# A token mixer in two groups of token tiles, with its sums added to u^T once a group

## The chip, the cores and the metric

The kernel runs on one core of a Trainium2 chip. The metric is device time in microseconds (us) of one execution, lower is better. Five engines work side by side, each through its own instructions in order: PE (TensorE, matrix products), DVE (VectorE), ACT (ScalarE), POOL (GpSimd) and SP (SyncE, which issues the transfers). They wait for each other on semaphores.

## The reference

Three stages follow each other. The first is a delta-rule attention over 768 tokens, 8 heads of width 48 and 4 batches; the other two work on its output `x` of shape (4, 768, 384):

```python
theta = x @ w_theta
zr, zi = x * np.cos(theta), x * np.sin(theta)
y = np.einsum('ts,bsd->btd', w_tok_r, zr) + np.einsum('ts,bsd->btd', w_tok_i, zi)
u = x + y
x = u + np.maximum(u @ w_ch, 0.0)
mu = np.mean(x, axis=-1, keepdims=True)
var = np.mean((x - mu) ** 2, axis=-1, keepdims=True)
xn = (x - mu) / np.sqrt(var + 1e-06) * g_ln
out = x + np.maximum(xn @ w_ch1, 0.0) @ w_ch2
```

The weights of the last two stages arrive in 64-bit floating point. Products are made in a 32-bit form that keeps fewer bits, so each operand is split into a high part and the rest (hi and lo), and three products (hi·hi, hi·lo, lo·hi) stand for one.

## The kernel before, in words

The attention takes the first 226 us. Then comes the mixing, 24 steps long. A step is one pair (batch b, token tile s) of the list `MIX`; a token tile is 128 tokens. The list goes through all six tiles of batch 0, then of batches 1, 2 and 3, the last one in the order 5, 4, 3, 2, 0, 1.

For a step, PE multiplies the tile's zr and zi (hi and lo) with the tile's token weights `w` and adds to six sums `y` in PSUM, three in each half of the step (L902 `mix`). A sum has 128 channels by 384 tokens; the six hold u^T of one batch. The sums of one batch run over its six steps. After the last of them DVE adds each to `uT` (L921), in which ACT has put x^T before (L849), and the next batch starts in the same three plus three PSUM buffers.

The preparation of later tiles runs ahead inside the step, between its halves: `theta(i+2)` on PE, `transpose(i+3)` on PE, `angles(i+2)` on DVE (`kk`, `nf`), `copies(i+3)` (`xh` on ACT, `xl` on DVE, x^T to `uT` on ACT), `sines` and `cosines` on ACT. At the start of step i, `turn(i+1)` makes the products with x (`zf`, one on POOL, one on DVE), the high parts `zh` (ACT) and the rest `zl` (POOL).

The same engines convert the 64-bit weights, half a token tile (a unit of 128 x 768) at a time, in the class `Weights`. A unit passes: transfer to `raw`, absolute value on ACT (L759), two instructions on DVE called the clamp here (L765, L766), two called the low pair (L775, L776), the cast of the high part on ACT (L789), and the subtraction for the low part (L794), which `add(..., split=)` gives to POOL or to DVE. `pump()` moves the units one stage on; the lists `PA` and `PB` say how many pumps a step makes, before its first and before its second half. In the first steps there are two a step, later one. Tiles 0 and 1 are loaded from late in the attention on, tiles 2 to 5 in steps 0 to 5, just ahead of their use. After them come twelve `stash` units (FFN weights, scaled by g on POOL and stored to DRAM), and `w_ch`.

The FFN stage takes eight halves j of a batch (384 tokens). Before half j can start, `pre(j)` runs eight pieces: `parts` (split of u), three `ch` (the w_ch product), `total`, `centre`, `square` with a second total, and `rstd`. For j = 0 they are placed in the mixing's last steps and the FFN's first ones, by the small dictionaries in the loop of `build`; the psum of a first product `ph` comes from the same buffers as the sums `y` of a step's first half.

Of the kernel before, what the change touches and what calls it, by code (L numbers as in the profile page):

```python
# [6 lines left out]
F32 = mybir.dt.float32  # L7
F32R = mybir.dt.float32r
# [3 lines left out]
ALU = mybir.AluOpType  # L12
# [650 lines left out]
C = 384  # L663
KB = 3
# [135 lines left out]
class Mixer:  # L800
# [19 lines left out]
    def load_w(self, s, wtok, pool, wts, w=None):  # L820
        w = self.W[s] = w or [pool.tile([128, 4, C], F32R, name=f"w{s}_{i}") for i in range(2)]
        for q in range(2):
            wts.add(("w", s, q), wtok[s, q], w[0][:, 2 * q:2 * q + 2], w[1][:, 2 * q:2 * q + 2])

    def trans(self, i):

# [11 lines left out]
    def copies(self, i, soon=1):  # L838
        nc = self.nc
        b, s = MIX[i]  # L840
        ps = self.XT
        xh = self.tp.tile([128, KB, 128], F32R, name="xh")
        xl = self.tp.tile([128, KB, 128], F32R, name="xl")
        nc.scalar.copy(out=xh, in_=ps)
        for k in range(2):
            if k == soon:
                nc.vector.tensor_tensor(out=xl, in0=ps, in1=xh.bitcast(F32), op=ALU.subtract)
            else:
                nc.scalar.copy(out=self.uT[b][:, :, 128 * s:128 * s + 128], in_=ps)  # L849
# [49 lines left out]

    def mix(self, i, half, yp):  # L900

        nc = self.nc  # L902
        b, s = MIX[i]
        zh, zl = self.Z[i]
        first, last = i % 6 == 0, i % 6 == 5
        qs = range(3 * half, 3 * half + 3)
        if first:
            for q in qs:
                self.Y[q] = yp.tile([128, C], F32, name="y", tag="h" if q < 3 else "acc")
        for ps in (((zh, 0), (zl, 0)), ((zh, 1),)):  # L910
            for q in qs:
                k, h = q // 2, q % 2
                for ri in range(2):
                    for l, w in ps:
                        nc.tensor.matmul(self.Y[q], l[:, ri, 128 * k:128 * k + 128], self.W[s][w][:, 2 * ri + h],  # L915
                                         start=(first and w == ri == 0 and l is zh), stop=(last and w == ri == 1))
        if last:
            for q in qs:
                k, h = q // 2, q % 2
                o = self.uT[b][:, k, C * h:C * h + C]  # L920
                nc.vector.tensor_tensor(out=o, in0=o, in1=self.Y[q], op=ALU.add)  # L921


class FFN:
# [24 lines left out]
    def pre(self, j, big, wp, psc):  # L949
# [54 lines left out]
        def rstd():  # L1004
            ps = bcast("v")
            t = lambda nm, p=wp: p.tile([128, N], F32, name=nm)
            v, a, y = t("v"), t("tot"), t("rs", self.rp)
            nc.vector.tensor_scalar(out=v, in0=ps, scalar1=1.0 / C, scalar2=1e-6, op0=ALU.mult, op1=ALU.add)
            nc.scalar.activation(out=y, in_=v, func=AF.Sqrt)
            nc.vector.reciprocal(out=y, in_=y)  # L1010
            nc.vector.scalar_tensor_tensor(out=a, in0=v, scalar=0.5, in1=y, op0=ALU.mult, op1=ALU.mult)
            nc.gpsimd.tensor_tensor(out=a, in0=a, in1=y, op=ALU.mult)
            nc.vector.scalar_tensor_tensor(out=y, in0=a, scalar=1.5, in1=y, op0=ALU.subtract, op1=ALU.mult)
            self.RS[j] = y
# [51 lines left out]
class Spare:  # L1066
# [5 lines left out]
    def tile(self, shape, dt, name):  # L1072
        if name == "tot":
            return self.st.tile([128, 2, C], dt, name="t", bufs=3)[:, 0]
        if self.n == 0:
            self.t = self.st.tile([128, 2 * C, 2], U32, name="raw", bufs=2).rearrange("p c t -> p (c t)")
        self.n += shape[1]
        return self.t[:, self.n - shape[1]:self.n].bitcast(dt)


def build(tc, a):
# [8 lines left out]
    with tc.manual_schedule(), outer:  # L1090
# [68 lines left out]
        wts.more = spare.enter_context(tc.tile_pool(name="st_more", bufs=1))  # L1159
        dp = outer.enter_context(tc.tile_pool(name="f_flat", bufs=1, space=bass.MemoryType.DRAM))  # L1160
        flat = {}
        for f in range(NF):
            flat[f] = dp.tile([128, 2, C], F32, name=f"flat{f}")
            wts.stash(("s", f), a["wff"][f], flat[f], g)

        def two_f(f, hi, lo):
            for n in range(2):
                ff.load_f(f + n, flat, hi[:, 2 * n:2 * n + 2], lo[:, 2 * n:2 * n + 2], wts)

        SLOTS = {"uh": 4, "ul": 5, "xh": 2, "xl": 3}  # L1170

        def big(nm, dt, j=0):
            if j % 2 == 0:
                return slot(f"{nm}", SLOTS[nm], [128, KB, N], dt)
            return xp_.tile([128, KB, N], dt, name=nm)

        n = len(MIX)
        PA = [2] + [1] * 23
        PB = [1] * 5 + [0] * 13 + [1] * 6
        wp = Late()  # L1180
        wp.pool = ff.sp = Spare(wts.st)
        todo = ff.pre(0, big, wp, psa)
# [107 lines left out]
```

## Time and profile before

| | |
|---|---|
| time, median of 3 runs | 798.16 us (795.78 to 798.22) |
| the profiled execution | 796.42 us, of which the span shown is 794.4 us |
| attention | 0 to 226.7 us |
| mixing, 24 steps | 226.7 to 448.8 us |
| FFN | 448.8 to 794.4 us |
| DVE busy over the span | 521.8 us (66%) |
| PE busy over the span | 715.5 us (90%) |

Times in rows are from the start of the span. A row of the timeline gives the start, the duration, the engine, the source line, the operation, the tiles (out<-in), the shape, and in brackets the idle time before it and who ended that. Rows that stand for several instructions in a run have x2 or x3 and give the time of all.

### The profile page before, as it was taken

How to read it: one execution, taken by the hardware profiler on the slowest of the kernel's cores; microseconds unless marked ns; L12 is line 12 of the kernel's file. 1: busy time of each engine (PE TensorE's matmuls, PEld its weight loads, DVE VectorE, ACT ScalarE, POOL GpSimd, SP SyncE). 2: the span in 40 equal slices, each digit the busy share in tenths (PEclk: the TensorE clock that was granted, in tenths of full speed). 3: DMA queues.
4: the chain of work that ended last, by engine and by line, in shares of the span. 5: the costliest groups of instructions: out<-in, count | busy, mean ns of one | idle time of the engine just before them, and what ended most of it. 6: DMA issues, size and time to landing. Idle time of an engine off the chain costs nothing.

```text
span 794.4 us, 19211 instructions
## 1 busy us (share of the span) xinstructions
PE 715.5 (90%) x8059; PEld 655.8 (83%) x8062; DVE 521.8 (66%) x835; ACT 347.0 (44%) x783; POOL 316.3 (40%) x311
## 2 busy tenths in 40 slices
PE   4687887777878788999999999999999999999997
PEld 2455555545567678999999999999999999999997
DVE  5899999985699999797843664535353443444342
ACT  1276776686865454555453434122223222231310
POOL 3755755643166766655634432313121112112120
PEclk7699999999999899999999999999999999999999
DMA  8776757324444332535301130000000000000000
GB/s 269 226 197 190 223 166 221 90 73 128 144 167 148 122 117 86 175 121 164 115 1 40 60 100 1 31 1 31 1 31 1 30 1 31 1 1 31 1 31 30
DMA packets 29718, 71.41 MB, mean 90 GB/s; under 512 B 4928, under 2 KB 17472, under 8 KB 29632
## 3 DMA queue, kind: packets, MB, share of 16 engines
q1 hardware_dynamic: 29632, 70.19, 28.2%
q8 instruction: 63, 1.03, 0.5%
q14 instruction: 23, 0.19, 0.1%
HBM read 56.02 MB, written 9.44 MB: 82 GB/s over the span
## 4 chain that ended last, share of the span: by engine, by line
PE 67%; DVE 17%; ACT 6%; issue 5%; POOL 3%; DMA 1%; SPq 1%; ACTq 0%; DVEq 0%; POOLq 0%
PE ph L1026 19%; PE acc L1045 19%; PE y L915 14%; PE pc L967 5%; DVE prod L356 3%; PE pth L859 3%; ACT bdw L439 3%; DVE t L775 2%; DVE XT L365 2%; DVE t L766 1%; DVE Ti L365 1%; DVE t L765 1%; PE py L473 1%; PE S L447 1%; DVE t L776 1%
## 5 line engine op out<-in xcount | busy, mean ns | idle before, releaser
L915 PE MATMUL y<-w,zh 128*128 128x384 f32 x576 | 157.6, 347 | 16.1 <-ACT w L789 12.4
L1045 PE MATMUL acc<-hh,f 128*128 128x384 f32 x576 | 147.0, 336 | 0.0
L1031 DVE SCALAR_TENSOR_TENSOR hl<-ph,hh 128x384 fp32r<-128x384 f32 x96 | 52.3, 553 | 108.2 <-ACT hh L1030 108.2
L915 PEld LDWEIGHTS y<-w,zh 128*128 128x128 f32 x576 | 107.2, 193 | 19.4 <-ACT w L789 14.4
L1030 ACT ACTIVATE hh<-ph 128x384 fp32r<-128x384 f32 x96 | 46.6, 491 | 161.0 <-PE ph L1026 161.0
L1026 PE MATMUL ph<-xh,f 128*128 128x384 f32 x576 | 116.4, 337 | 0.0
L1045 PEld LDWEIGHTS acc<-hh,f 128*128 128x128 f32 x576 | 104.4, 188 | 0.0
L1026 PEld LDWEIGHTS ph<-xh,f 128*128 128x128 f32 x576 | 101.8, 188 | 0.4 <-issue 0.3
L915 PE MATMUL y<-w,zl 128*128 128x384 f32 x288 | 98.7, 343 | 0.0
L1045 PE MATMUL acc<-hl,f 128*128 128x384 f32 x288 | 97.0, 337 | 0.0
L897 POOL TENSOR_TENSOR zl<-zf,zh 128x384 fp32r<-128x384 f32 x48 | 65.8, 1391 | 41.5 <-ACT zh L896 41.5
L1026 PE MATMUL ph<-xl,f 128*128 128x384 f32 x288 | 65.7, 336 | 0.0
L439 ACT COPY bdw<-RW 32x192 f32<-32x192 f32 x192 | 59.6, 310 | 11.5 <-PE RW L435 7.2
L915 PEld LDWEIGHTS y<-w,zl 128*128 128x128 f32 x288 | 55.5, 193 | 0.0
L452 ACT COPY bds<-S 48x384 f32<-48x384 f32 x92 | 43.6, 474 | 26.7 <-PE S L447 25.4
L447 PE MATMUL S<-bdw,ktt 128*48 128x192 f32 x368 | 41.2, 347 | 15.4 <-ACT bdw L439 15.4
L1055 POOL TENSOR_TENSOR o<-u,o 128x384 f32<-128x384 f32 x21 | 20.8, 1020 | 84.9 <-DVE o L1054 84.9
L1045 PEld LDWEIGHTS acc<-hl,f 128*128 128x128 f32 x288 | 54.0, 188 | 0.3 <-DVE hl L1031 0.3
L1026 PEld LDWEIGHTS ph<-xl,f 128*128 128x128 f32 x288 | 51.6, 188 | 0.0
L447 PEld LDWEIGHTS S<-bdw,ktt 128*48 128x48 f32 x368 | 20.5, 127 | 29.9 <-ACT bdw L439 23.7
L974 POOL TENSOR_TENSOR tot<-uh 128x384 f32<-128x384 f32 x8 | 8.4, 1052 | 92.1 <-ACT uh L1001 87.2
L435 PEld LDWEIGHTS RW<-Rs,pt 32*32 32x32 f32 x1472 | 19.4, 107 | 30.4 <-DVE Rs L427 23.7
(149 smaller groups left out, 1367.0 us busy)
## 6 DMA issues: line engine op xcount, KB each, us to landing
kqt<-kq SPq DMA_DIRECT2D x20, 512.0 KB, 5.2
raw<-wtok SPq DMA_DIRECT2D x12, 768.0 KB, 4.4
raw<-wff SPq DMA_DIRECT2D x12, 768.0 KB, 4.9
bdk<-kq SPq DMA_DIRECT2D x40, 192.0 KB, 3.9
vt<-vin SPq DMA_DIRECT2D x24, 192.0 KB, 3.8
ktt<-ktok SPq DMA_DIRECT2D x24, 192.0 KB, 4.8
x<-ys SPq DMA_DIRECT2D x96, 48.0 KB, 2.5
flat<-t SPq DMA_DIRECT2D x12, 384.0 KB, 5.5
```

The source lines that it names most:

```text
L356: eng.tensor_tensor(out=pr[:, j], in0=bc(lhs[:, j].unsqueeze(2), [128, i, c, kk]), in1=bc(rhs[:, j].unsqueeze(1), [128, i, c, kk]), op=ALU ...
L365: v.tensor_reduce(out=o, in_=pr, axis=AX.X, op=ALU.add, negate=neg)
L439: nc.scalar.copy(out=b[rr, :, r, :], in_=RW[h][rr, 1, :, :])
L447: nc.tensor.matmul(S_ps[h][64 * e:64 * e + D, g, :], KT[c][:, 2 * h + g, e, :], b[:, 2 * g + e, :, :], start=(c == 0 and g == 0), stop=Tru ...
L452: nc.scalar.copy(out=n[ee, :, e, :], in_=S_ps[h][ee, :, :].rearrange("p g (r d) -> p (g r) d", r=4))
L897: nc.gpsimd.tensor_tensor(out=zl[:, q], in0=zf[:, q], in1=zh[:, q].bitcast(F32), op=ALU.subtract)
L915: nc.tensor.matmul(self.Y[q], l[:, ri, 128 * k:128 * k + 128], self.W[s][w][:, 2 * ri + h], start=(first and w == ri == 0 and l is zh), st ...
L967: nc.tensor.matmul(ps, self.wc[w][:, k, 128 * e:128 * e + 128], r[:, k], start=(n == 0), stop=(n == 8))
L1026: nc.tensor.matmul(ps, w[:, 0, 128 * k:128 * k + 128], r[:, k], start=(n == 0), stop=(n == 8))
L1030: nc.scalar.activation(out=hh, in_=ps, func=AF.Relu)
L1031: nc.vector.scalar_tensor_tensor(out=hl, in0=ps, scalar=0.0, in1=hh.bitcast(F32), op0=ALU.max, op1=ALU.subtract)
L1045: nc.tensor.matmul(self.ACC[j][e], w[:, 1, 128 * e:128 * e + 128], r, start=(f == 0 and n == 0), stop=(f == NF - 1 and n == 2))
```

## The change

The list `MIX` goes through tiles 0 to 2 of all four batches first (steps 0 to 11), then through tiles 3 to 5 (steps 12 to 23, in the last batch as 5, 4, 3). The sums of a batch now run over three steps and are put to `uT` twice, eight times in all. In the first group the token half that has x^T already (h = 0) is added by DVE, the other one is copied by ACT. For tiles 3 to 5, x^T is added to `uT` by DVE (L852 of the new file), where ACT wrote it before. The low parts of tiles 0 to 2 are made by DVE alone. One step fewer has two pumps at the start. `pre(0)`, whose batch is finished after step 14, moves forward to steps 15 to 22 as a whole, and tiles for it and for the FFN's first weights take other buffers.

```diff
-MIX = [(b, s) for b in range(3) for s in range(6)] + [(3, s) for s in (5, 4, 3, 2, 0, 1)]
+MIX = [(b, s) for b in range(4) for s in range(3)] + [(b, s) for b in range(3) for s in (3, 4, 5)] + [(3, s) for s in (5, 4, 3)]
...
-            wts.add(("w", s, q), wtok[s, q], w[0][:, 2 * q:2 * q + 2], w[1][:, 2 * q:2 * q + 2])
+            wts.add(("w", s, q), wtok[s, q], w[0][:, 2 * q:2 * q + 2], w[1][:, 2 * q:2 * q + 2], split=0 if s < 3 else None)
...
+            u = self.uT[b][:, :, 128 * s:128 * s + 128]
             if k == soon:
                 nc.vector.tensor_tensor(out=xl, in0=ps, in1=xh.bitcast(F32), op=ALU.subtract)
+            elif s < 3:
+                nc.scalar.copy(out=u, in_=ps)
             else:
-                nc.scalar.copy(out=self.uT[b][:, :, 128 * s:128 * s + 128], in_=ps)
+                nc.vector.tensor_tensor(out=u, in0=u, in1=ps, op=ALU.add)
...
-        first, last = i % 6 == 0, i % 6 == 5
+        first, last = i % 3 == 0, i % 3 == 2
...
-                nc.vector.tensor_tensor(out=o, in0=o, in1=self.Y[q], op=ALU.add)
+                if s < 3 and h:
+                    nc.scalar.copy(out=o, in_=self.Y[q])
+                else:
+                    nc.vector.tensor_tensor(out=o, in0=o, in1=self.Y[q], op=ALU.add)
...
-            v, a, y = t("v"), t("tot"), t("rs", self.rp)
+            v, a, y = t("v"), t("tot"), t("rs", self.rp if j else self.rp0)
...
-        SLOTS = {"uh": 4, "ul": 5, "xh": 2, "xl": 3}
+        SLOTS = {"uh": 2, "ul": 3, "xh": 0, "xl": 1}
...
-        PA = [2] + [1] * 23
-        PB = [1] * 5 + [0] * 13 + [1] * 6
+        PA = [2] + [1] * 21 + [2] * 2
+        PB = [1] * 4 + [0] * 14 + [1] * 4 + [2] * 2
...
-            if i + 1 == n - 1:
-                todo[4]()
...
-            for k in {20: (1,), 21: (2,)}.get(i, ()):
+            for k in {16: (1,), 17: (2,), 18: (3,)}.get(i, ()):
                 todo[k]()
...
+                stash(range(6, NF))
-            if i == 18:
+            if i == 21:
                 two_f(0, *[slot(f"f0_{k}", 6 + k, [128, 4, C], F32R) for k in range(2)])
-            if i == 21:
-                two_f(2, *[slot(f"f2_{k}", k, [128, 4, C], F32R) for k in range(2)])
-            for k in {19: (0,), 21: (3,), 22: (5,)}.get(i, ()):
+            if i == 22:
+                two_f(2, *[slot(f"f2_{k}", 4 + k, [128, 4, C], F32R) for k in range(2)])
+            for k in {15: (0,), 19: (4,), 20: (5,), 21: (6,), 22: (7,)}.get(i, ()):
                 todo[k]()
...
-            if i == 0:
-                last[6]()
-            if f == 3:
+            if j and f == 3:
                 last[7]()
```

DVE's order at the start of the mixing. Before, in steps 0 and 1 (`zf..x1_70` is tile 1's product with x; t_4167 and t_4293 are the two units of `w` tile 1, t_4303 is the first of tile 2):

```order
L894 TENSOR_TENSOR zf_4173<-zf_4173,x1_70 128x384
L775 SCALAR_TENSOR_TENSOR t_4167<-raw_4032,t_4167 128x768
L776 SCALAR_TENSOR_TENSOR t_4167<-raw_4032,t_4167 128x768
L765 TENSOR_SCALAR t_4293<-t_4293 128x768
L766 TENSOR_SCALAR t_4293<-t_4293 128x768
L775 SCALAR_TENSOR_TENSOR t_4293<-raw_4171,t_4293 128x768
L776 SCALAR_TENSOR_TENSOR t_4293<-raw_4171,t_4293 128x768
L765 TENSOR_SCALAR t_4303<-t_4303 128x768
L766 TENSOR_SCALAR t_4303<-t_4303 128x768
```

The same place now (t_4287 is tile 1's second unit, t_4297 the first of tile 2):

```order
L897 TENSOR_TENSOR zf_4173<-zf_4173,x1_70 128x384
L775 SCALAR_TENSOR_TENSOR t_4167<-raw_4032,t_4167 128x768
L776 SCALAR_TENSOR_TENSOR t_4167<-raw_4032,t_4167 128x768
L794 TENSOR_TENSOR w1_1_3699<-t_4167,w1_0_3698 128x768
L765 TENSOR_SCALAR t_4287<-t_4287 128x768
L766 TENSOR_SCALAR t_4287<-t_4287 128x768
L775 SCALAR_TENSOR_TENSOR t_4287<-raw_4171,t_4287 128x768
L776 SCALAR_TENSOR_TENSOR t_4287<-raw_4171,t_4287 128x768
L794 TENSOR_TENSOR w1_1_3699<-t_4287,w1_0_3698 128x768
L765 TENSOR_SCALAR t_4297<-t_4297 128x768
L766 TENSOR_SCALAR t_4297<-t_4297 128x768
```

Each unit's subtraction (L794) came from POOL to DVE, right behind the low pair whose result ACT must cast in between; the same happens twice more for tile 2.

DVE's order where the mixing ends. Before, from the centring of half 0 (`ul`, `xl`) to the FFN's first `hl` (u_4240 is batch 3's `uT`, to which the mixing's last sums go):

```order
L994 SCALAR_TENSOR_TENSOR ul<-pst,u_65 128x384
L934 TENSOR_TENSOR xl<-ul,xh 128x384
L794 TENSOR_TENSOR f_1_6157<-t,f_0_6156 128x384
L921 TENSOR_TENSOR u_4240<-u_4240,y 128x384 x3
L794 TENSOR_TENSOR f_1_6157<-t,f_0_6156 128x384
L921 TENSOR_TENSOR u_4240<-u_4240,y 128x384 x3
L979 TENSOR_TENSOR sl<-tot,sh 128x384
L1031 SCALAR_TENSOR_TENSOR hl<-ph,hh 128x384 x3
```

Now, from the end of the centring (before step 21's products) to the same `hl`:

```order
L942 TENSOR_TENSOR xl<-ul,xh 128x384
L897 TENSOR_TENSOR zf<-zf,x_2921 128x384
L987 TENSOR_TENSOR raw<-t,raw 128x384
L897 TENSOR_TENSOR zf<-zf,x_72 128x384
L794 TENSOR_TENSOR f_1_6225<-t,f_0_6224 128x384 x2
L1016 TENSOR_SCALAR raw<-pst 128x384
L1018 RECIPROCAL rs<-rs 128x384
L1019 SCALAR_TENSOR_TENSOR t<-raw,rs 128x384
L1021 SCALAR_TENSOR_TENSOR rs<-t,rs 128x384
L929 TENSOR_TENSOR u_4240<-u_4240,y 128x384 x3
```

The centring stands ahead of the products of the last two tiles, and the whole of `rstd` ahead of the last sums' way to `uT`.

## Rows read from the trace of the kernel before

**Rows 1.** Stretches: length, busy PE, PEld, DVE, ACT, POOL, clock, DMA, GB/s.
```profile
235.00:300.00 65.00, 48.45 (x242) 44.42 (x240) 63.93 (x64) 32.24 (x56) 43.82 (x25) 0.92 0.35 123
257.30:270.40 13.10, 10.19 (x49) 9.55 (x48) 12.89 (x13) 6.40 (x12) 8.96 (x6) 0.87 0.33 122
300.00:349.00 49.00, 49.00 (x289) 48.78 (x290) 41.59 (x56) 24.74 (x48) 29.65 (x26) 1.00 0.42 129
414.00:449.00 35.00, 34.22 (x198) 33.61 (x197) 16.10 (x28) 13.29 (x26) 12.41 (x11) 1.00 0.07 23
449.00:794.40 345.40, 341.13 (x1947) 339.80 (x1946) 156.69 (x270) 91.39 (x178) 69.01 (x67) 1.00 0.07 24
```

**Rows 2.** Timeline of PE: two waits in the mixing, and the FFN's first product.
```profile
247.61 0.44 PE L915 MATMUL y<-w,zh 128*128 128x384 f32 x1 [1.74 <-ACT w L789]
...
300.00 0.41 PE L915 MATMUL y<-w,zh 128*128 128x384 f32 x1 [3.05 <-DVE u L921]
...
448.84 1.30 PE L1026 MATMUL ph<-xh,f 128*128 128x384 f32 x6
```

**Rows 3.** Timeline of DVE, from one product zf to the next, step 2.
```profile
254.90 0.55 DVE L894 TENSOR_TENSOR zf<-zf,x 128x384 f32<-128x384 f32 x1
...
256.54 1.65 DVE L775 SCALAR_TENSOR_TENSOR t<-raw,t 128x768 uint32<-128x768 uint32 x1
...
259.79 2.17 DVE L765 TENSOR_SCALAR t<-t 128x768 f32<-128x768 f32 x1
261.99 2.07 DVE L766 TENSOR_SCALAR t<-t 128x768 uint32<-128x768 uint32 x1
...
265.50 0.95 DVE L775 SCALAR_TENSOR_TENSOR t<-raw,t 128x768 uint32<-128x768 uint32 x1
...
268.06 0.55 DVE L894 TENSOR_TENSOR zf<-zf,x 128x384 f32<-128x384 f32 x1
```

**Rows 4.** Timeline of POOL in the same steps.
```profile
237.40 1.87 POOL L794 TENSOR_TENSOR w<-t,w 128x768 fp32r<-128x768 f32 x1 [3.34 <-ACT w L789]
...
256.12 2.93 POOL L897 TENSOR_TENSOR zl<-zf,zh 128x384 fp32r<-128x384 f32 x2 [1.96 <-ACT zh L896]
259.01 4.63 POOL L794 TENSOR_TENSOR w<-t,w 128x768 fp32r<-128x768 f32 x2
```

**Rows 5.** Timeline of ACT: a unit's cast, and the two casts zh.
```profile
236.50 0.83 ACT L789 CAST w<-t 128x768 fp32r<-128x768 f32 x1 [2.14 <-DVE t L776]
...
268.69 0.93 ACT L896 CAST zh<-zf 128x384 fp32r<-128x384 f32 x2 [1.07 <-DVE zf L894]
```

**Rows 6.** Timeline of DVE in steps 6 to 11, with one pump a step.
```profile
311.47 0.56 DVE L894 TENSOR_TENSOR zf<-zf,x 128x384 f32<-128x384 f32 x1 [1.32 <-POOL zf L893]
...
319.32 0.56 DVE L894 TENSOR_TENSOR zf<-zf,x 128x384 f32<-128x384 f32 x1 [1.32 <-POOL zf L893]
...
347.81 1.47 DVE L921 TENSOR_TENSOR u<-u,y 128x384 f32<-128x384 f32 x3
```

**Rows 7.** Timeline of DVE, the end of the attention.
```profile
217.50 0.56 DVE L894 TENSOR_TENSOR zf<-zf,x 128x384 f32<-128x384 f32 x1 [3.48 <-ACT zf L884]
...
227.46 0.56 DVE L847 TENSOR_TENSOR xl<-pt,xh 128x384 fp32r<-128x384 f32 x1 [1.34 <-ACT xh L844]
```

**Rows 8.** Timeline of DVE, the end of the mixing and pre(0).
```profile
418.24 2.59 DVE L794 TENSOR_TENSOR f<-t,f 128x384 fp32r<-128x384 f32 x2 [1.79 <-ACT f L789]
...
442.58 0.56 DVE L994 SCALAR_TENSOR_TENSOR ul<-pst,u 128x384 f32<-128x384 f32 x1 [3.20 <-PE pst L985]
...
446.94 0.56 DVE L934 TENSOR_TENSOR xl<-ul,xh 128x384 fp32r<-128x384 f32 x1 [0.58 <-ACT xh L933]
...
448.15 1.48 DVE L921 TENSOR_TENSOR u<-u,y 128x384 f32<-128x384 f32 x3
...
456.00 0.56 DVE L1008 TENSOR_SCALAR v<-pst 128x384 f32<-128x384 f32 x1 [0.37 <-PE pst L985]
...
461.49 1.35 DVE L1013 SCALAR_TENSOR_TENSOR rs<-tot,rs 128x384 f32<-128x384 f32 x1 [1.20 <-POOL tot L1012]
```

More of the change, by code (lines that the diff above doesn't have):

```diff
@@ L1074, in tile @@
             return self.st.tile([128, 2, C], dt, name="t", bufs=3)[:, 0]
-        if self.n == 0:
+        if self.n % (4 * C) == 0:
+            self.n = 0
             self.t = self.st.tile([128, 2 * C, 2], U32, name="raw", bufs=2).rearrange("p c t -> p (c t)")
@@ L1161, in build, with stash @@
         flat = {}
-        for f in range(NF):
-            flat[f] = dp.tile([128, 2, C], F32, name=f"flat{f}")
-            wts.stash(("s", f), a["wff"][f], flat[f], g)
+        def stash(fs):
+            for f in fs:
+                flat[f] = dp.tile([128, 2, C], F32, name=f"flat{f}")
+                wts.stash(("s", f), a["wff"][f], flat[f], g)
+        stash(range(6))
         def two_f(f, hi, lo):
@@ L1168, in two_f @@
                 ff.load_f(f + n, flat, hi[:, 2 * n:2 * n + 2], lo[:, 2 * n:2 * n + 2], wts)
-        SLOTS = {"uh": 4, "ul": 5, "xh": 2, "xl": 3}
+        SLOTS = {"uh": 2, "ul": 3, "xh": 0, "xl": 1}
+        soon = {"uh": 0, "ul": 1}
         def big(nm, dt, j=0):
+            if nm in soon and todo is first_pre:
+                return mx.cst.tile([128, KB, N], dt, name=nm, tag=f"w0_{soon[nm]}")
             if j % 2 == 0:
@@ L1177, in build @@
         n = len(MIX)
-        PA = [2] + [1] * 23
-        PB = [1] * 5 + [0] * 13 + [1] * 6
+        PA = [2] + [1] * 21 + [2] * 2
+        PB = [1] * 4 + [0] * 14 + [1] * 4 + [2] * 2
         wp = Late()
         wp.pool = ff.sp = Spare(wts.st)
-        todo = ff.pre(0, big, wp, psa)
+        todo = first_pre = ff.pre(0, big, wp, psa)
+        ff.rp0 = lp
         mx.trans(DELAY)
@@ L1217, in build @@
                 ff.load_ch(a["wch"], outer.enter_context(tc.tile_pool(name="wch", bufs=1)), wts)
-            if i == 18:
+                stash(range(6, NF))
+            if i == 21:
                 two_f(0, *[slot(f"f0_{k}", 6 + k, [128, 4, C], F32R) for k in range(2)])
-            if i == 21:
-                two_f(2, *[slot(f"f2_{k}", k, [128, 4, C], F32R) for k in range(2)])
-            for k in {19: (0,), 21: (3,), 22: (5,)}.get(i, ()):
+            if i == 22:
+                two_f(2, *[slot(f"f2_{k}", 4 + k, [128, 4, C], F32R) for k in range(2)])
+            assert i < 15 or ("c", 2) in wts.ready, wts.todo
+            for k in {15: (0,), 19: (4,), 20: (5,), 21: (6,), 22: (7,)}.get(i, ()):
                 todo[k]()
```

## The prediction, made before the changed kernel ran

> **What bounds the kernel now.** I read the stretches by stage first, then PE's timeline for the waits, then the queues of DVE, POOL and ACT around them. From 300 us on PE is full: six steps take 49.00 us with PE busy for all of it, 8.17 us a step, and the FFN's 345.40 us are full as well [rows 1]. What can be won lies in steps 1 to 5, from 235 to 300 us: 65.00 us for five steps, of which PE would need 5 x 8.17 = 40.8. The prize is 24.2 us, including the 3.05 us that PE waits at 300.00 for DVE to add batch 0's sums to u^T [rows 2].
>
> PE's waits there name a weight cast on ACT (1.74 us at 247.61), which invites the thought that tiles 3 to 5 come too late. But the reader is to see who feeds ACT: DVE is busy for 63.93 of the 65.00 us [rows 1]. ACT waits for DVE's low pair [rows 5]. So it is DVE's queue, in order, that sets these steps; one step of it takes 268.06 - 254.90 = 13.16 us [rows 3]. A part of that is POOL's doing: a clamp instruction takes 2.17 and 2.07 us while POOL subtracts weights and 0.55 us otherwise, a low instruction 1.65 us beside zl and 0.95 us alone [rows 3, 4]. PE's later use of w moves; DVE's queue stays ahead of each tile's zf, zl, theta and of the sums' adds. Where the list now defers a weight, PE waits for those instead.
>
> **Term 1, DVE's queue up to step 6.** I add up what stands between zf of tile 1 and the first add of step 5's sums, which lets PE into step 6 (300.0 us before).
>
> Steps 0 and 1. Four subtractions come to DVE. Each has two inputs of 128x768, as a low instruction has: 0.95 us [rows 3], 3.8 in all. One of them (tile 2's first) falls under zl on POOL and waits for about one half of it: +1.0. A subtraction needs ACT's cast of what DVE has just made, with nothing of DVE between: 0.83 us and the hand-over, 0.9, for three of them; for tile 2's first, zf stands between, so ACT has the two zh casts (0.93) to do before: 1.75 [rows 5]. That is 4.45 us of waiting. In return POOL has no weights to subtract, so clamp pairs go at 1.1 us where 4.24 were paid [rows 3]; two such pairs stand here: -6.2. Sum: 3.8 + 1.0 + 4.45 - 6.2 = +3.05. For the price of one such subtraction the trace holds another row: two of 128x384 beside POOL took 2.59 us [rows 8], or 2.6 for one of 128x768; I take the 0.95, as POOL idles beside three of the four.
>
> The Trainium skill, "SBUF — State Buffer", section "Who interferes with whom", says that the port pair which DVE and POOL share is held for a whole instruction and the other one blocks until its end. By that the subtraction under zl costs the rest of one zl and its own 0.95, about 2 us and not 2.6; the sum would be the same as above, and 0.65 us more by the row.
>
> Step 2. It is now the last of a group: three adds to u^T come into DVE's queue, two ahead of the next clamp, at 1.47/3 = 0.49 us each [rows 6], +1.4. Since that clamp then overlaps less of POOL's two subtractions, -0.9. Sum +0.5. Step 3: the same 13.16 us as before. Step 4 has one pump now: a clamp pair under POOL (4.24) and a low pair (2.6) go, but POOL still subtracts both units of tile 5 (4.63) behind zl (2.93) before it makes the next zf, on which DVE's waits; POOL's chain of 1.2 + 2.93 + 4.3 + 1.0 gives 9.45 us, so -3.7 and not -6.8 [rows 4]. Step 5: the first add comes as late behind zf as before.
>
> Sum 3.05 + 0.5 - 3.7 = -0.15 us. PE enters step 6 at about 299.9: of the prize nothing is left. Bounds: -6 if the 4.45 us of waiting and the rest of POOL's chain were covered, +7 if each subtraction cost 2.6.
>
> **Term 2, more adds in steps 6 to 15.** With one pump DVE's loop takes 319.32 - 311.47 = 7.85 us against PE's 8.17, with 1.32 us of it idle [rows 6]. Every third step gains adds. In the first group two stand ahead of kk (+0.94), the third in the idle time: 3 x 7.85 + 0.94 = 24.5 for PE's 24.5. In the second group x^T's add takes 0.47 of the idle time, three adds stand ahead of kk (1.4) and three behind, 0.55 of which doesn't fit: 25.5 for 24.5. From step 16 to 18 the ch products (nine matmuls, 1.57 us each) lengthen PE's steps and pay that back. I take +0.3, bounds 0 and +3 (1.0 for each of three groups). ACT's copies cost nothing: ACT is busy for 24.74 of 49.00 us [rows 1].
>
> **Term 3, pre(0) inside the last steps.** Before, its pieces met a DVE with 16.10 busy us of 35.00 [rows 1], and centre, square and rstd stood behind the last zf. Now four places press:
> - ch(0) in step 16 needs uh and ul, which queue on ACT behind cos and on DVE behind step 15's weights; about 1.6 us late for PE, where the same place cost 0.95 before. +0.65.
> - centre starts when PE has pst and holds DVE from 442.58 to 447.50, 4.9 us [rows 8]; behind it now stands tile 22's zf, and zl is ready 4.15 us after it (254.90 to 259.05, rows 3, 4), for a step of 7.9. About +0.5.
> - Tile 23's zf waits for sl, that for POOL's two totals, those for ACT's square: zl about +1.2 late.
> - rstd takes 456.00 to 462.84, 6.8 us [rows 8], and stands ahead of the last sums' adds, behind two f subtractions (2.59). PE's last step takes 6.4 us and then wants the buffer that the first add frees; before, the add was at 448.15 and the product at 448.84 [rows 2, 8]. About +1.7.
>
> Sum +4.05; bounds 0 (all found slack) and +8 (each twice).
>
> **Nothing from the attention.** The two subtractions of tile 0 come to DVE there; the queue has 3.48 us idle before 217.50 and 1.34 before 227.46 [rows 7], and one 0.95 with its 0.9 wait goes into each, the second by virtue of clamps that POOL no longer slows. Bounds 0 and +1.5. The FFN stays PE's.
>
> **Sum.** -0.15 + 0.3 + 4.05 = +4.2 us, made on the profiled execution, 796.42 us, which is 1.7 us under the median of 798.16: **800.6 us**.
>
> **Rivals.**
> - *The weights were the wait* (faster). PE's waits do name the cast; if DVE's queue has room once the tiles are due later, PE gets back the three waits of 2.9 us with the slow clock around them (0.87 granted in 257.3 to 270.4, rows 1) and a part of 3.05: 13 us, less term 3's 4: 787. Against it: 63.93 of 65.00 busy.
> - *The first steps gain a little, and pre(0) fits.* Term 1 at -4, term 3 at +1: 793.5. For it: DVE's idle times at the end; against it: the queue order is fixed.
> - *No net change.* Term 1 as summed, term 3 at a quarter: 797.5.
> - *PE's clock falls at group ends* (slower). Eight group ends instead of four, each with PE waiting for an add; where PE waited some 3 us in steps 3 to 5 the granted clock was 0.87 [rows 1] and a step lost 13.1 - 8.17 - 2.9 = 2 us more. With DVE's loop as the pace in four second-group steps and such a loss at each: +4.2 + 4 x 2 = 808. It decides once DVE starts a group's last step more than 2.7 us behind PE: its first add comes 0.5 + 1.1 + 3.4 + 0.5 = 5.5 us after zf (zf, clamp, low pair under zl, add), and PE needs the buffer 8.17 us after its own start.
>
> **How the numbers follow.** The forecast of term sums near +4 has 0.48; the clock rival 0.06; no net change 0.26; the small gain 0.13; the weights rival 0.07. A measurement of this kernel tells 0.3% (2.4 us) from no change. Slower by more than that: the forecast's own cases but for a part near +2.4 (0.45) and the clock, 0.51. Same: 0.29. Faster: 0.20. The forecast's own range is 798 to 804; for eight in ten I reach to the small gain and half of the clock rival, 792 to 807.
>
> **What would show it.** Right: DVE over 95% busy from 235 to about 285 us; DVE idle for about 0.9 us ahead of each new L794, ended by ACT w; PE entering step 6 between 298 and 302 us after a wait for DVE's u; PE waiting for zl in steps 22 or 23 and for DVE's u at the FFN's start. Wrong: steps 3 to 5 at 8.2 us each, or PE entering step 6 before 296; PE full from step 15 to the FFN would take away term 3.

## The result and the profile after

The kernel takes 806.2 us (median of 7 runs, 803.06 to 807.67) where the one before takes 798.16 (7 runs, 795.68 to 800.77): a ratio of 1.0099, 95% interval 1.0073 to 1.0125. It is slower by 1.0%. The forecast was 800.6 us with a range of 792 to 807. The direction and the range hold; the loss is 8.0 us where 4.2 were summed from the profiled execution. The profiled execution after takes 804.83 us, of which the span is 802.6.

A stage is cut here at the start of PE's first `y` product of a step: steps 0 to 6, steps 7 to 15, steps 16 to 23 up to the first `ph`, and the FFN. First the stages of before, which overlap [rows 1]; columns as there.

```profile
226.66:308.23 81.57, 65.02 (x339) 60.92 (x337) 79.46 (x82) 40.80 (x71) 53.53 (x32) 0.94 0.37 131
381.61:448.84 67.23, 66.45 (x387) 65.70 (x387) 35.91 (x60) 29.92 (x60) 29.38 (x26) 1.00 0.13 42
```

Then the same stretches of the kernel after, with parts of them.

```profile
235.00:285.00 50.00, 37.66 (x175) 35.38 (x176) 45.66 (x53) 24.95 (x45) 23.24 (x15) 0.86 0.32 112
225.00:306.07 81.07, 65.68 (x336) 62.68 (x337) 70.43 (x82) 41.92 (x76) 42.07 (x27) 0.92 0.39 135
...
306.07:379.46 73.39, 73.39 (x433) 72.97 (x433) 64.85 (x91) 37.73 (x73) 43.78 (x36) 1.00 0.37 113
...
379.46:458.36 78.90, 72.22 (x389) 68.75 (x389) 51.98 (x82) 31.32 (x57) 34.09 (x32) 0.96 0.24 80
...
379.46:395.15 15.69, 12.25 (x58) 11.16 (x58) 13.50 (x22) 6.56 (x13) 6.61 (x6) 0.89 0.53 154
...
390.06:395.15 5.09, 5.09 (x21) 5.09 (x22) 4.22 (x8) 2.04 (x4) 1.40 (x2) 0.66 0.88 244
447.40:452.30 4.90, 4.21 (x13) 3.45 (x14) 3.18 (x4) 3.64 (x5) 4.53 (x4) 0.65 0.11 21
...
458.36:802.61 344.25, 340.06 (x1945) 339.74 (x1945) 151.93 (x266) 88.83 (x174) 65.74 (x63) 1.00 0.06 20
```

Steps 0 to 6 take 81.07 us for 81.57, so -0.5; steps 7 to 15 take nine times 8.15, as before; the last eight steps take 78.90 for 67.23, so +11.7; the FFN 344.25 for 345.53, so -1.3. With the mixing starting 1.7 us earlier the span grows by 8.2. That start lay between 223.4 and 228.4 us over all the profiles, whatever the edit, so the 1.7 is no gain of the change: from the mixing's start to the end it costs 9.9 us (577.6 for 567.7). The whole loss lies in steps 16 to 23, where PE had been full: clock 1.00 and 66.45 of 67.23 busy before.

Now PE's waits there. Timeline of PE after, steps 6, 16, 23 and the FFN's start; the bracket is idle time and who ended it.

```profile
298.48 0.44 PE L920 MATMUL y<-w,zh 128*128 128x384 f32 x1 [1.82 <-DVE u L929]
...
383.17 1.79 PE L975 MATMUL pc<-uh,wc 128*128 128x384 f32 x6 [0.42 <-ACT uh L941]
...
385.32 1.20 PE L862 MATMUL pth<-tw,xh 128*128 128x384 f32 x6
...
390.06 0.55 PE L835 MATMUL pt<-ident,x 128*128 128x128 f32 x3 [3.02 <-DVE u L977]
...
390.63 0.53 PE L920 MATMUL y<-w,zl 128*128 128x384 f32 x1
390.95 0.53 PE L920 MATMUL y<-w,zh 128*128 128x384 f32 x1
...
447.40 0.45 PE L920 MATMUL y<-w,zh 128*128 128x384 f32 x1 [0.62 <-ACT zh L899]
448.48 0.59 PE L920 MATMUL y<-w,zl 128*128 128x384 f32 x1 [0.63 <-POOL zl L900]
...
458.36 0.93 PE L1034 MATMUL ph<-xh,f 128*128 128x384 f32 x4 [1.72 <-DVE u L929]
```

The costliest row of the last steps is that of L835. It is a transpose of x (`pt`, step 19's token tile), and what releases it is DVE's add of the ch product to u. It has nothing to do with u. But `pt`, `pth` and `pc` are tiles of one PSUM tag, "pa", with two buffers: `pt` takes the buffer of `pc`, and that is free only when the add has read it. Behind the wait the products come every 0.32 us (390.63, 390.95) where they come every 0.174 us at full clock; the stretch has 0.66 granted, between the two levels of 1.2 and 2.4 GHz. The six uh products at 383.17 take 1.79 us for 1.20 at a granted clock of 1.00 (383.17 to 384.80); there PE waits for ACT's three casts of uh one by one. Where DVE is meanwhile (timeline of DVE, after: the first steps, step 16, and the end of the mixing):

```profile
231.95 0.96 DVE L794 TENSOR_TENSOR w<-t,w 128x768 fp32r<-128x768 f32 x1 [2.92 <-ACT w L789]
...
236.85 0.96 DVE L794 TENSOR_TENSOR w<-t,w 128x768 fp32r<-128x768 f32 x1 [0.90 <-ACT w L789]
...
245.21 1.71 DVE L794 TENSOR_TENSOR w<-t,w 128x768 fp32r<-128x768 f32 x1 [1.78 <-ACT w L789]
...
383.15 1.50 DVE L942 TENSOR_TENSOR ul<-u,uh 128x384 fp32r<-128x384 f32 x3 [1.18 <-ACT uh L941]
384.56 0.55 DVE L897 TENSOR_TENSOR zf<-zf,x 128x384 f32<-128x384 f32 x1
385.03 0.55 DVE L765 TENSOR_SCALAR t<-t 128x768 f32<-128x768 f32 x1
385.62 0.56 DVE L766 TENSOR_SCALAR t<-t 128x768 uint32<-128x768 uint32 x1
386.21 1.66 DVE L775 SCALAR_TENSOR_TENSOR t<-raw,t 128x768 uint32<-128x768 uint32 x1
387.90 1.63 DVE L776 SCALAR_TENSOR_TENSOR t<-raw,t 128x768 uint32<-128x768 uint32 x1
389.46 0.54 DVE L977 SCALAR_TENSOR_TENSOR u<-pc,u 128x384 f32<-128x384 f32 x1
...
445.48 0.81 DVE L987 TENSOR_TENSOR raw<-t,raw 128x384 fp32r<-128x384 f32 x1 [7.04 <-ACT raw L986]
...
448.53 2.56 DVE L794 TENSOR_TENSOR f<-t,f 128x384 fp32r<-128x384 f32 x2 [1.78 <-ACT f L789]
...
452.14 2.55 DVE L1018 RECIPROCAL rs<-rs 128x384 f32<-128x384 f32 x1 [0.59 <-ACT rs L1017]
...
457.68 1.47 DVE L929 TENSOR_TENSOR u<-u,y 128x384 f32<-128x384 f32 x3
```

PE had turned from the product to `pth` at 385.32. The add stood behind a clamp and a low pair, in program order, and ran at 389.46. At the end the reciprocal and what follows stand ahead of the last three adds, the first of which lets PE start the FFN.

### The profile page after: what moved, and what is told of

It is laid out like the page before. It is cut to its first block, busy times and chain, and to the rows that moved or that the text cites. A ratio compares the mean times of both kernels' runs of the same rounds, so it can differ in the third digit from the quotient of the medians.

```text
span 802.6 us, 19216 instructions
## 1 busy us (share of the span) xinstructions
PE 718.3 (89%) x8059; PEld 658.3 (82%) x8062; DVE 527.6 (66%) x865; ACT 347.2 (43%) x783; POOL 302.7 (38%) x305
## 4 chain that ended last, share of the span: by engine, by line
PE 53%; DVE 26%; ACT 8%; issue 6%; POOL 5%; DMA 1%; SPq 0%; ACTq 0%; DVEq 0%; POOLq 0%
PE ph L1034 19%; PE acc L1053 19%; PE pc L975 5%; DVE t L775 4%; PE y L920 4%; DVE t L776 3%; DVE prod L356 3%; ACT bdw L439 2%; DVE t L766 2%; DVE XT L365 2%; DVE t L765 2%; PE pth L862 1%; DVE zf L897 1%; POOL prodp L372 1%; POOL prodp L356 1%
## 5 line engine op out<-in xcount | busy, mean ns | idle before, releaser
L920 PE MATMUL y<-w,zl 128*128 128x384 f32 x288 | 101.1, 351 | 1.0 <-POOL zl L900 0.6
L920 PEld LDWEIGHTS y<-w,zl 128*128 128x128 f32 x288 | 57.2, 199 | 2.6 <-POOL zl L900 2.6
L896 POOL TENSOR_TENSOR zf<-zf,x 128x384 f32<-128x384 f32 x24 | 27.4, 1141 | 73.3 <-ACT zf L879 73.2
L435 PEld LDWEIGHTS RW<-Rs,pt 32*32 32x32 f32 x1472 | 19.4, 107 | 30.8 <-DVE Rs L427 24.2
```

## The experiments

All times are ratios to the kernel before, run on the same chip; diffs are against the kernel after unless said otherwise. In an expectation "theory" is the account as it stood before that run.

**Which part costs: all of pre(0) late again (e1).** The pieces of pre(0) stand where before had them.

```diff
+            if i + 1 == n - 1:
+                todo[4]()
...
-            for k in {16: (1,), 17: (2,), 18: (3,)}.get(i, ()):
+            for k in {20: (1,), 21: (2,)}.get(i, ()):
...
-            for k in {15: (0,), 19: (4,), 20: (5,), 21: (6,), 22: (7,)}.get(i, ()):
+            for k in {19: (0,), 21: (3,), 22: (5,)}.get(i, ()):
...
+            if i == 0:
+                last[6]()
-            if j and f == 3:
+            if f == 3:
```

> Only the places of pre(0) are undone: its eight pieces stand again where they stood before the change, from step 19 into the FFN. Theory (pre(0) inside the last steps costs the time, through DVE's queue): the 11 us that the mixing lost between step 16 and the FFN's first product go, so the time falls by 9 to 12 us, to 794 to 797, level with the kernel before or up to 1% under it; step 16 takes 8.2 us. Rival (the second group's extra adds to u^T on DVE, and one more single-pump step, are what slows the last steps): the stalls move with DVE's lag and at most 3 us are won, 803 or more.

Measured 794.31 us (10 runs), ratio 0.9967 (0.9942 to 0.9991). The windows of its steps 0 to 6, and of steps 16 to 23 up to the first `ph`:

```profile
224.69:306.71 82.02, 63.95 (x337) 60.21 (x337) 71.92 (x84) 42.07 (x76) 42.80 (x28) 0.94 0.39 133
380.09:446.18 66.09, 66.09 (x388) 65.91 (x388) 46.16 (x76) 27.91 (x54) 30.46 (x27) 1.00 0.25 78
```

The last steps are full and 12.8 us shorter, of which 1.3 come back in the FFN (345.59 us for 344.25). So the place of pre(0) is the loss; all else that the change does is worth 0.3%, in its favour.

**Only the end late (e2).** Square, total and rstd go back into the FFN; split, ch and centre stay early.

```diff
-            for k in {15: (0,), 19: (4,), 20: (5,), 21: (6,), 22: (7,)}.get(i, ()):
+            for k in {15: (0,), 19: (4,), 20: (5,)}.get(i, ()):
...
+            if i == 0:
+                last[6]()
-            if j and f == 3:
+            if f == 3:
```

> Only square with its total and rstd go back to the FFN's first products, as before the change; parts, ch, total and centre stay in steps 15 to 20. Theory: the waits for zl in step 23, the slow clock after them and the wait of 1.72 us before the FFN's first product go, some 5 us (step 22 at 6.6, step 23 at 6.4, no wait at the FFN's start); step 16 keeps its 15.7 us; 800 to 802. Rival (DVE's earlier work, the centring, sets the end of the mixing): under 2 us are won, 804 or more.

Measured 799.41 us (10 runs, ratio 1.0034, 1.0012 to 1.0055), just under the 800 to 802 expected. Steps 16 to 23 up to the first `ph`:

```profile
379.47:452.27 72.80, 69.15 (x388) 67.31 (x388) 48.77 (x82) 28.64 (x54) 31.46 (x29) 0.98 0.23 71
```

No wait is left at the FFN's start. So of the 12.8 us some 6.1 are square, total and rstd at the end. Of the other 6.7, 6.05 are ch(0) in step 16, which takes 15.76 us here too, with 2.99 us for L977, where e1 has 9.71 for a step with one ch product.

**What holds the buffer: no pump in steps 15 and 16 (e3).** The clamp and low pair ahead of the add are gone there and come later.

```diff
-        PA = [2] + [1] * 21 + [2] * 2
+        PA = [2] + [1] * 14 + [0] * 2 + [1] * 5 + [2] * 2
```

> Steps 15 and 16 make no pump, so four of DVE's weight instructions a step (4.5 us) leave its queue there; the units come two steps later. Theory (the add of the first w_ch product stands behind a late DVE queue, and the transposition waits for that PSUM buffer): step 16 falls from 15.7 to 10 to 10.7 us, the time by 4 to 6, to 800 to 802. Rival (PE waits for ACT's uh, behind cos): the 0.4 us stall ahead of the product was that wait, the rest stays: 804 or more.

Measured 804.02 us (4 runs), ratio 1.0085 (1.0053 to 1.0116). Step 16 takes 9.72 us without a wait, as the theory has it; the total missed. Steps 16 to 23 take 74.93 us for 78.90, so 4.0 less and not 6, as step 18 takes 11.53 us (9.93 in the kernel after): PE waits 1.59 us there, since the third ch product's add meets the same queue (DVE below). The rest of the miss lies elsewhere: in this profile the mixing starts 3.3 us later than in that of the kernel after, and the FFN takes 345.63 us for 344.25.

```profile
406.27 1.65 DVE L776 SCALAR_TENSOR_TENSOR t<-raw,t 128x768 uint32<-128x768 uint32 x1
...
409.41 0.55 DVE L977 SCALAR_TENSOR_TENSOR u<-pc,u 128x384 f32<-128x384 f32 x1
```

**The pump behind the cosines (e9).** From step 4 to 17 the step's pump stands behind angles, copies and cosines; from 18 on as it was.

```diff
-        PA = [2] + [1] * 21 + [2] * 2
-        PB = [1] * 4 + [0] * 14 + [1] * 4 + [2] * 2
+        PA = [2] + [1] * 3 + [0] * 14 + [1] * 4 + [2] * 2
+        PB = [1] * 22 + [2] * 2
...
-            for _ in range(PB[i]):
+            for _ in range(PB[i] if PA[i] else 0):
                 wts.clamps()
```

> The changed kernel with one move: from step 4 to step 17 the step's single pump (clamp and low pair on DVE) stands behind the angles, copies and cosines of the step, where it stood before its first half. Theory (order in DVE's queue): the add u<-pc of ch(0) and the sums' adds no longer wait behind a clamp and a low pair, the PE wait of 3.02 us at 390.06 in step 16 and its slow clock go: step 16 falls from 15.7 to 9.7 to 10.2 us, the total by 5 to 7 us, to 799 to 801; step 23 and the FFN's start keep their +5. Rival (the amount of DVE work in the steps with ch pieces sets it, in whatever order): step 16 or 17 stays above 12 us, 804 or more.

Measured 802.19 us (10 runs), ratio 1.0081 (1.0047 to 1.0115). Steps 16 and 17, where no pump stands ahead, take 9.95 and 9.71 us. In step 18 a pump stands ahead again, and so does the wait. PE there, then DVE:

```profile
407.39 0.55 PE L835 MATMUL pt<-ident,x 128*128 128x128 f32 x3 [2.99 <-DVE u L977]
...
407.95 0.34 PE L920 MATMUL y<-w,zl 128*128 128x384 f32 x1
408.13 0.34 PE L920 MATMUL y<-w,zh 128*128 128x384 f32 x1
```

```profile
402.36 0.56 DVE L765 TENSOR_SCALAR t<-t 128x768 f32<-128x768 f32 x1
...
405.23 1.63 DVE L776 SCALAR_TENSOR_TENSOR t<-raw,t 128x768 uint32<-128x768 uint32 x1
406.79 0.55 DVE L977 SCALAR_TENSOR_TENSOR u<-pc,u 128x384 f32<-128x384 f32 x1
```

One kernel thus has both cases side by side: without the four instructions ahead of the add no wait, with them 2.99 us. The total of 799 to 801 missed by a little. In the profile step 18 takes 12.91 us for the 9.93 of the kernel after, and the FFN 347.09 for 344.25, since its first products get half the clock. PE's first FFN product here, then the windows of 4.9 us from step 23's start and of the FFN's start:

```profile
454.46 2.26 PE L1034 MATMUL ph<-xh,f 128*128 128x384 f32 x6 [2.91 <-DVE u L929]
```

```profile
443.51:448.41 4.90, 3.91 (x19) 3.34 (x20) 3.18 (x4) 3.64 (x5) 4.55 (x4) 1.00 0.13 24
454.46:460.00 5.54, 5.54 (x17) 5.54 (x18) 3.67 (x8) 0.49 (x1) 0.24 (x1) 0.50 0.00 0
```

**The buffer alone (e10).** ACT reads the product out of PSUM, and DVE's queue stays as it is.

```diff
-            nc.vector.scalar_tensor_tensor(out=u[:, e], in0=ps, scalar=0.0, in1=u[:, e], op0=ALU.max, op1=ALU.add)
+            if j == 0:
+                if "r" not in hold:
+                    hold["r"] = big("pr", F32)
+                nc.scalar.activation(out=hold["r"][:, e], in_=ps, func=AF.Relu)
+                nc.vector.tensor_tensor(out=u[:, e], in0=u[:, e], in1=hold["r"][:, e], op=ALU.add)
+            else:
+                nc.vector.scalar_tensor_tensor(out=u[:, e], in0=ps, scalar=0.0, in1=u[:, e], op0=ALU.max, op1=ALU.add)
...
+            if nm == "pr":
+                return mx.cst.tile([128, KB, N], dt, name=nm, tag="w1_0")
```

> The changed kernel with one edit: for pre(0) ACT takes the positive part of each ch product out of PSUM into an SBUF tile, and DVE adds that tile to u^T where it added the product before; DVE's order and every pump stay. Theory (PE's 3.02 us wait in step 16 is for the PSUM buffer that DVE's add holds behind a clamp and a low pair): the buffer comes free from ACT, the wait and its slow clock go, step 16 falls from 15.7 to 10 to 12 us, total 800 to 803. Rival (DVE's queue itself is late, through the angles and the product zf, whatever the buffer): PE waits as long in step 16 or 17 for something else of DVE's, 804 to 808.

Its window of step 16, then DVE and PE there:

```profile
379.52:389.49 9.97, 9.92 (x59) 9.60 (x59) 8.65 (x14) 5.41 (x11) 5.04 (x4) 1.00 0.47 127
```

```profile
386.49 1.65 DVE L776 SCALAR_TENSOR_TENSOR t<-raw,t 128x768 uint32<-128x768 uint32 x1
388.06 0.55 DVE L981 TENSOR_TENSOR u<-u,pr 128x384 f32<-128x384 f32 x1
```

```profile
385.98 0.55 PE L835 MATMUL pt<-ident,x 128*128 128x128 f32 x3
```

DVE's add stands as far back in the queue as before, behind the same low pair, and runs at 388.06, 8.5 us after the step's start (10.0 in the kernel after); PE's transpose runs 2.1 us ahead of it. Step 16 takes 9.97 us and steps 16 to 23 take 73.62 instead of 78.90. So it is the buffer and not DVE's lateness as such. From the mixing's start to the end this profile takes 573.0 us, where the kernel after takes 577.6. In time this is less plain: the profiled execution took 799.51 us, the median of six runs 803.95 (ratio 1.009, 1.0062 to 1.0119), which can't be told from the kernel after. The stages of the other runs were not recorded; the mixing's start alone differs by 5 us over the profiles. Why four of the six took about 804 stays open.

**Term 1, the subtractions on DVE (e4, e7).** The low parts of tiles 0 to 2 go back to POOL as before: in the kernel after (e4), and with e1's late pre(0) (e7).

```diff
-            wts.add(("w", s, q), wtok[s, q], w[0][:, 2 * q:2 * q + 2], w[1][:, 2 * q:2 * q + 2], split=0 if s < 3 else None)
+            wts.add(("w", s, q), wtok[s, q], w[0][:, 2 * q:2 * q + 2], w[1][:, 2 * q:2 * q + 2])
```

> Only the low parts of tiles 0 to 2 go back from DVE to POOL. By my sum of DVE's queue, four subtractions with their waits for ACT cost 9.25 us and save 6.2 of contention: without them step 2 is entered about 3 us earlier and the time is 2 to 4 us lower, 802 to 804. Rival (POOL was the worse place, the contention dominates): the first steps get slower, 808 or more. A third outcome, no change, means that PE's entry into step 6 is set by POOL's chain behind tile 5.

> pre(0) at its old places and the low parts of tiles 0 to 2 on POOL, two pumps in steps 0 to 3: apart from the buffers this is the group order with its adds and one double-pump step less, against the kernel before. Theory: the group order alone gains little, as DVE's queue up to step 6 loses one unit (3.7 us by POOL's chain) and gains the adds: 791 to 795, some 1 to 2 us under the one with DVE's low parts. Rival (the casts' waits were hidden, DVE's low parts cost nothing): the same as that one, 794 to 795.

Measured e4 804.38 us (1.0081, 1.0052 to 1.0109) and e7 790.3 us (0.9918, 0.9883 to 0.9954). Steps 0 to 6 take 79.71 and 77.21 us, so 1.4 less than in the kernel after and 4.8 less than in e1. One profile each is little for this: both have the same code up to step 14 and yet differ by 2.5 us, and five profiles with the subtractions on DVE (after, e1, e2, e3, e10), again with the same code there, lie between 80.45 and 82.02. On the mean the two take 2.8 us less than the five, near the +3.05 summed for steps 0 and 1. In total time e4, 0.4 us over the expected 802 to 804, can't be told from the kernel after; e7 lies 0.7 us under the expected 791 to 795.

**Is there a better version (e5, e6, e8, e11, e12)?** With the tiles due later, two pumps a step are not needed for so long. e5 is e1 with

```diff
-        PB = [1] * 4 + [0] * 14 + [1] * 4 + [2] * 2
+        PB = [1] * 2 + [0] * 16 + [1] * 4 + [2] * 2
```

and e6 adds e7's move to POOL.

> pre(0) at its old places, and besides two pumps a step only in steps 0 and 1, as tile 3 is due at step 12 now. Theory (DVE's queue of weight work sets steps 1 to 5, not the due time of a weight): two units of 7 us leave the queue ahead of step 6 and go to steps 19 and 20, where DVE has room, so steps 2 to 6 shorten by 5 to 9 us in all against the same kernel without it; 785 to 790. Rival (the group end's adds and POOL's chain set the entry into step 6 whatever the pumps do): 792 or more.

> As the one before, and the low parts of tiles 0 to 2 on POOL again. Theory: DVE no longer waits for ACT's casts in steps 0 to 2, and PE's wait of some 5 us for tile 2's second unit (with the slow clock behind it) falls to under 2: 1 to 4 us less than that kernel, 783 to 788. Rival (with fewer pumps the contention with POOL counts more): as much or more than that kernel.

Measured e5 793.3 us (0.9953, 0.993 to 0.9975) and e6 788.37 us (0.9889, 0.9853 to 0.9925), each over what was expected, e6 by 0.4 us; PE's wait for tile 2's second unit fell from 5.02 us in e5 to 1.77 in e6. Windows of e6: steps 0 to 6, and step 20.

```profile
223.41:291.57 68.16, 60.16 (x336) 56.55 (x337) 60.59 (x71) 38.77 (x71) 46.06 (x29) 1.00 0.35 119
400.77:415.95 15.18, 12.88 (x58) 11.22 (x59) 12.83 (x22) 6.49 (x14) 8.58 (x8) 0.89 0.30 105
```

The first steps gain 13.4 us against before, a little over half of the prize of 24.2. But the units left over then come through DVE in steps 19 and 20 too, where e1 has none, ahead of uh and ul, and step 20 takes 15.2 us where e1 has 9.7. For e5 that was not expected, and it missed: its first steps shortened by more than the 5 to 9 us of the theory, but its time is that of the rival.

Three kernels tried to get this back. e8 is e6 with the pump behind the cosines from step 2 on; e11 is e6 with that in steps 19 and 20 alone; e12 is e6 with the split of u a step earlier.

```diff
# e8 against e6
-        PA = [2] + [1] * 21 + [2] * 2
-        PB = [1] * 2 + [0] * 16 + [1] * 4 + [2] * 2
+        PA = [2] + [1] * 1 + [0] * 16 + [1] * 4 + [2] * 2
+        PB = [1] * 22 + [2] * 2
...
-            for _ in range(PB[i]):
+            for _ in range(PB[i] if PA[i] else 0):
                 wts.clamps()
# e11 against e6: that last line as well, and
-        PA = [2] + [1] * 21 + [2] * 2
-        PB = [1] * 2 + [0] * 16 + [1] * 4 + [2] * 2
+        PA = [2] + [1] * 18 + [0] * 2 + [1] * 1 + [2] * 2
+        PB = [1] * 2 + [0] * 16 + [1] * 1 + [2] * 2 + [1] * 1 + [2] * 2
# e12 against e6
-            for k in {19: (0,), 21: (3,), 22: (5,)}.get(i, ()):
+            for k in {18: (0,), 21: (3,), 22: (5,)}.get(i, ()):
```

> The changed kernel with pre(0) at before's places, the low parts of tiles 0 to 2 back on POOL, two pumps only in steps 0 and 1, and from step 2 on the single pump behind the angles, copies and cosines instead of before the first half. Theory (order in DVE's queue): the chain angles, sine, product and the sums' adds no longer stand behind the low pair; DVE's loop falls from 7.85 to about 6.5 us, the late steps 14 and 17 to 19 go back to 8.2 us and step 20 from 15.2 to about 9.7: 779 to 783. Rival (the amount of DVE work, not its order, sets those steps): 787 or more.

> The kernel with pre(0) at before's places, low parts of tiles 0 to 2 on POOL and two pumps only in steps 0 and 1, with one move: in steps 19 and 20 the pumps stand behind the cosines. Theory: in step 20 the angles no longer stand behind a clamp and a low pair, ACT's uh comes 4 us earlier, step 20 falls from 15.2 to 9.7 to 11 us, total 782 to 785. Rival (step 20 is late for what DVE has left over from steps 17 to 19, where a pump moved behind the cosines only moves the lag into step 21): 787 or more.

> The kernel with pre(0) at before's places, low parts of tiles 0 to 2 on POOL and two pumps only in steps 0 and 1, with one move: parts (the split of u into uh and ul) at the end of step 18 in place of step 19. Theory (step 20 is long because ch(0) waits 2.57 us for uh or ul, which stand late in ACT's and DVE's queues, and the slow clock follows): with a whole step between parts and ch(0) no wait is left there and step 20 falls from 15.2 to 9.7 to 11 us, total 782 to 785. Rival (DVE's queue is full in steps 17 to 20, so that the three subtractions of parts only move the lag into step 19, or the add that follows the product comes as late): 787 or more.

Measured e8 788.61 us (0.9892, 0.9855 to 0.9928), e11 789.57 (0.9913, 0.9884 to 0.9942) and e12 790.57 (0.9913, 0.9885 to 0.9942): none better than e6, and each in the range of the rival. e8 does free steps 14 and 17 to 18 (8.15 us each), but step 20 takes 16.2. In e12 the wait only changes its name (the 2.57 us of its expectation are e5's; in e6, from which it starts, ch(0) waits 1.02 us). PE at the start of its step 20:

```profile
406.69 0.45 PE L920 MATMUL y<-w,zh 128*128 128x384 f32 x1 [2.90 <-ACT zh L899]
```

Here the three ul subtractions stand ahead of DVE's zf, on which zh and zl wait. What DVE must do in those steps, not its order alone, sets them. The best version measured is e6, 1.1% faster than before; e8 can't be told from it.

## Why the prediction was right, and where its size was off

**DVE's queue bounds the first steps: held.** e5 and e6 took work out of that queue, and steps 0 to 6 fell by 11.2 and 13.9 us against e1.

**Term 1, -0.15 us: measured -0.5, which is less than profiles of the same code differ by (80.45 to 82.02 us).** PE's wait for DVE's first add of step 5's sums ends 73.48 us after the mixing's start (298.48 - 225.00), where it ended 73.34 after it (300.00 - 226.66) [rows 2]. PE's entry into step 6, at 295.80, lies under the 296 that I had named as a sign of being wrong. The mixing had begun 1.7 us earlier, and the wait for u now stands inside step 6 and not at its entry.

The term's pieces show in the rows: the wait for the cast is 0.90 us as put for the second units of tiles 1 and 2, and 1.78 for tile 2's first unit, where 1.75 was put. For tile 1's first unit it is 2.92 where 0.9 was put: ahead of that cast ACT had the absolute value of the next unit, and for this it waited 2.86 us on the transfer. A subtraction alone takes 0.96 (0.95 put), the one under zl 1.71. First ACT's row, then POOL's:

```profile
230.29 0.90 ACT L759 ACTIVATE t<-raw 128x768 f32<-128x768 f32 x1 [2.86 <-DMA raw<-wtok]
...
244.10 2.00 POOL L900 TENSOR_TENSOR zl<-zf,zh 128x384 fp32r<-128x384 f32 x2 [1.96 <-ACT zh L899]
```

The Trainium skill, "SBUF — State Buffer", section "Who interferes with whom", has the other engine blocked to the end of the instruction; this row agrees within 0.15 us, as zl has 0.89 us left when the subtraction starts at 245.21, and with its own 0.96 that makes 1.85. The 2.6 us of the nearest row did not come.

One sign was wrong: I said DVE would be busy over 95% of 235 to 285 us. It is 91%, and in steps 0 to 6 it is busy for 70.43 us, where before it was for 79.46. The change took nine busy microseconds from DVE and gave it 6.5 us of waiting for ACT's four casts, where before it had none; the stage stayed as it was. The 4.45 us of waiting in the term's own sum already contradicted that sign.

**Term 2, +0.3 us: measured 0.** Steps 7 to 15 take 73.39 us for 73.38.

**Term 3, +4.05 us: measured +11.7, beyond its bound of +8, less the 1.3 by which the FFN is shorter. This is the term that was mis-sized.** By its places:

- *ch(0) in step 16, +0.65 put: +5.0 net.* Step 16 takes 15.69 us for the 9.71 of a step with one ch product and no wait, which is 5.98 too much; before, the same product cost 0.94 too much in step 20. I saw uh's lateness, and it is there with 1.0 us (0.42 ahead of the six products and 0.6 within them). I followed the product's inputs in DVE's and ACT's queues, but not its output: the two-buffer tag, and a full DVE queue behind which the buffer is given back. That is 3.02 us, and some 1.6 us of slow clock come behind it (twelve products, most at 0.32 us for 0.174). e9 and e10 show it from both sides.
- *Centre, +0.5, tile 23's zf, +1.2, and rstd ahead of the last adds, +1.7: together +6.05.* Step 22 takes 8.14 us for 6.59, each with two products of a total, and step 23 takes 10.96 for 6.46. In step 23 PE waits 0.62 and 0.63 us for zh and zl, as named, gets 0.65 of the clock over 4.9 us, and waits 1.72 us at the end. That the last agrees with the 1.7 is luck: in e9 the same step has the clock at 1.00 and takes 10.95 us, with 2.91 us of waiting at its end. In both, DVE's first add comes 12.2 us after the subtraction of L987 (445.48 to 457.68; in e9 441.58 to 453.77). So DVE's queue sets this step, and the slow clock only takes the place of a part of the wait. I had put rstd's 6.8 us and the two f subtractions into that queue, but not the 1.78 us that DVE waits for ACT's cast of f ahead of them, though its like stands in the row [rows 8]. The remaining 0.9 us of the difference stay open.
- *The rest, about +0.6:* the two products of the first total, which now stand in step 20 (8.50 us for 8.15), and 0.2 us in step 18.

**The rivals.** That the weights were the wait, and that pre(0) fits, fall with the windows. The clock rival's time, 808, came nearer than 800.6, but not by its mechanism: its place was the group ends of the second group, four with 2 us of slow clock each. Behind the ends after steps 14, 17 and 20 the steps lose 0.2 us or nothing, and behind the last PE has its clock (1.00 from 458.36 on). At the end after step 5 PE waits 1.82 us and step 6 takes 10.27, no more than that wait and 0.3 us over 8.15; steps 7 to 15, three group ends among them, lose nothing.

**The chances.** Slower had 0.51 and came true, with the time 0.8 us under the range's upper edge. Which engine sets the last steps was right; what stayed narrow was Term 3, whose bound of +8 ("each twice") doubled the waits that I had found and left no room for one that I had not.

## What to carry to other kernels

When work is moved into a stretch where PE is full, follow its PSUM tile to its release as well as its inputs to their arrival: the reader of that tile stands in some engine's queue, and the next tile of the same tag, whatever it computes, waits for it. A queue that keeps up on average may still hold four instructions ahead of the one that frees a buffer, and here such a wait of some 3 us cost PE 3.2 us in one kernel (step 18 of e9) and 5.0 in another (step 16 of the kernel after, without the 1.0 for uh). Where one engine's work bounds a stage, giving it a piece that waits for another engine's answer can turn busy time into idle time and leave the stage as long as it was, as in steps 0 to 6 here.

## What the runs showed of the hardware

Waits of one length had different prices. Behind 3.02 us of waiting in step 16 of the kernel after, the products came at 0.32 us each (0.66 granted from 390.06 to 395.15). Behind 2.99 us in step 18 of e9 the very next ones came at 0.174 us (1.00 granted from 407.39 to 412.00), with a step of 12.91 us, just the wait and 0.2 us over 9.71. It is not the short wait for uh that tells the two apart. e4 has none: PE was busy for all of 306.00 to 378.51 us, in step 16 it has this one wait, and behind it the clock falls all the same. Its row and its window:

```profile
387.69 0.55 PE L835 MATMUL pt<-ident,x 128*128 128x128 f32 x3 [2.77 <-DVE u L977]
```

```profile
387.69:392.76 5.07, 5.07 (x21) 5.07 (x22) 4.21 (x8) 2.04 (x4) 1.39 (x2) 0.66 0.82 242
```

Even steps with the same code and the same waits got either clock. In step 4 of e1 and of e3 PE waits 0.8 us for zl and then 3.30 us for DVE's nf; e1 first:

```profile
273.35:286.09 12.74, 8.82 (x48) 7.96 (x48) 12.57 (x12) 6.46 (x11) 8.60 (x6) 1.00 0.35 122
276.08:291.49 15.41, 11.34 (x49) 10.63 (x49) 15.17 (x15) 6.76 (x12) 11.27 (x7) 0.78 0.31 110
```

What tells the cases apart no run here shows. Nor does the slow clock cost time wherever it comes: over steps 4 to 6, where DVE's queue sets the pace, e1 takes 34.3 us and e3 32.7, and step 23 takes 10.95 us in e9 at full clock and 10.96 in the kernel after, with 0.65 granted over its first 4.9 us.
